# Block solve in four strips of 32 partitions, its scratch in longer runs, and two transfers per pair of head groups, under a new order

## The chip, the core and the metric

The kernel runs on one core of a Trainium2 chip. The metric is the device time of one execution in microseconds; lower is better. Five engines work side by side: PE (TensorE matmuls, with its weight loads shown as PEld), DVE (VectorE), ACT (ScalarE), POOL (GpSimd), and SP, which here only issues DMAs. ACT issues some DMAs too. [...]

## What is computed

```python
for t in range(S):                                  # 768 steps, for 4 x 8 heads of width 40
    y[:, :, t] = einsum('bhd,bhde->bhe', rt, state)
    Sa = einsum('bhde,bhe->bhd', state, at)
    state_decay = state * wt[:, :, None, :] - einsum('bhd,bhe->bhde', Sa, bt)
    state = state_decay + einsum('bhd,bhe->bhde', vt, kt)
x = y.transpose(0, 2, 1, 3).reshape(B * S, H * D)   # 3072 x 320
h = maximum(x @ moe_w_in, 0);  x = (h * h) @ moe_w_out          # 320 -> 2048 -> 320
h = x @ moe2_w_in;  out = where(h > 0, h, exp(min(h, 0)) - 1) @ moe2_w_out
```

All of it is float32: a recurrence over time, then two MLPs.

## The kernel before, in words

**Chunks.** Time is cut into 12 chunks of 64 steps. A chunk's recurrence is done with matrices: `scan`, `prep_a`, `prep_r` and `kb_rows` scale the inputs by running products of w; `planes` and `gram` make a 64 x 64 matrix for each of the 32 heads; the **solve** inverts it; `dyn_f`, `dyn_u`, `dyn_bu`, `dyn_s`, `dyn_y` apply it and carry the state on. Heads go in four groups of eight (`u` = 0 to 3) and two pairs of groups (`p`). The 256 rows of a chunk's y then go through the first MLP (`gemm1` writes `h`, `gemm2` writes `accA` and `accB`), and after the last chunk the second MLP runs chunk by chunk. Values for the MLPs are split into a high and a low part, so each product takes several matmuls: 224 for a chunk and an MLP, 5376 in all. The weights of the first MLP come in 24 pieces (`cs<-w`) that DVE, ACT and PE (`wl`) convert.

**The solve.** A 64 x 64 matrix is inverted by blocks of 16. `gram` stores it to DRAM (`b_scr`, one DMA from ACT for each u). `block_load` (line 997) reads the 128 diagonal blocks, one on each partition (tile `tt`). `block_step` (1009) runs 15 times, two DVE instructions each. `block_store` (1016) sends the inverses through DRAM: transposed through `n_scr` into `nt`, plain through `t_scr` into `tb`. `block_join` (1030) makes the off-diagonal blocks of each 32 x 32 with two stages of 64 small matmuls: stage one `join<-nt,pb` (16 rows, 32 columns, 16 moving), stage two `join<-tb,pb` (32 rows, 16 columns, 16 moving). Each is a float32 matmul, which the trace shows as two instructions with a weight load each, so a stage shows as x128. Stage one's tiles begin at partitions 0 and 32, stage two's at 0 and 32 for half of the heads and at 64 and 96 for the others. Copies on ACT and DVE take the results out of PSUM.

**The order.** No engine's order stands in the text as such. `at` (755) puts each step on a list with a time from three tables (`OFF` by step, `SHIFT` by stage and chunk, `BIAS` by step and chunk); `play` (759) and the class `Order` then lay all instructions out engine by engine with a cost model, the ready instruction of the lowest time first, and `emit` (523) issues them in that order. So every instruction of the main part has line 528 in the profile, and groups are told apart by tile names. Each engine runs its list strictly in order, and a DMA that waits on SP holds up the DMAs behind it.

Of the kernel before, what the change touches and what calls it, by code (L numbers as in the profile page):

```python
# [1459 lines left out]
```

## Time and profile before

| | us |
|---|---|
| median of 3 runs (lowest to highest) | 1325.73 (1323.58 to 1325.76) |
| the profiled execution, its own time | 1321.71 |
| its span, first to last instruction | 1319.9 |
| PE busy in it | 1207.2 |
| mean granted clock of TensorE | 0.949 |

The profiled execution is one run beside the three; its span is 1.8 us shorter than its time and lies inside it. [...]

### The profile page before, as it was taken

How to read it: one execution, taken by the hardware profiler on the slowest of the kernel's cores; microseconds unless marked ns; L12 is line 12 of the kernel's file. 1: busy time of each engine (PE TensorE's matmuls, PEld its weight loads, DVE VectorE, ACT ScalarE, POOL GpSimd, SP SyncE). 2: the span in 40 equal slices, each digit the busy share in tenths (PEclk: the TensorE clock that was granted, in tenths of full speed). 3: DMA queues.
4: the chain of work that ended last, by engine and by line, in shares of the span. 5: the costliest groups of instructions: out<-in, count | busy, mean ns of one | idle time of the engine just before them, and what ended most of it. 6: DMA issues, size and time to landing. Idle time of an engine off the chain costs nothing. (4 is left out here: it accounts for less than half of the span.)

```text
span 1319.9 us, 41548 instructions
## 1 busy us (share of the span) xinstructions
PE 1207.2 (91%) x17409; PEld 1105.7 (84%) x17409; DVE 769.4 (58%) x1434; ACT 792.5 (60%) x1536; POOL 510.3 (39%) x485
## 2 busy tenths in 40 slices
PE   2648779999998999999999999999999999999996
PEld 1536657889897898889888999999999999999995
DVE  6467866756575668665655645578744444444442
ACT  4556576565674657575655546455666666666663
POOL 2341241153363334364334224367633333333332
PEclk9996768897998799999999999999999999999998
DMA  8787786575777475765565434334200010000000
GB/s 268 189 222 207 179 253 153 126 187 150 185 195 164 104 203 130 196 138 160 129 160 136 103 77 135 123 103 124 65 21 20 22 30 21 21 21 22 16 11 18
DMA packets 239570, 157.99 MB, mean 120 GB/s; under 512 B 164112, under 2 KB 212624, under 8 KB 239376
## 3 DMA queue, kind: packets, MB, share of 16 engines
q1 hardware_dynamic: 213072, 148.18, 42.2%
q10 hardware_dynamic: 26304, 7.08, 2.8%
q8 instruction: 139, 2.28, 0.7%
q14 instruction: 55, 0.45, 0.1%
HBM read 114.52 MB, written 40.69 MB: 118 GB/s over the span
## 5 line engine op out<-in xcount | busy, mean ns | idle before, releaser
L528 PE MATMUL h<-xhi,w 128*128 128x256 f32 x1920 | 512.3, 298 | 2.9 <-DVE r L528 1.6
L528 POOL TENSOR_TENSOR glo<-r,ghi 128x512 fp32r<-128x512 f32 x192 | 254.0, 1324 | 413.9 <-ACT ghi L528 219.6
L528 PEld LDWEIGHTS h<-xhi,w 128*128 128x128 f32 x1920 | 357.8, 191 | 22.8 <-DVE r L528 12.7
L528 PE MATMUL h<-xlo,w 128*128 128x256 f32 x1152 | 324.4, 284 | 1.8 <-POOL xlo L528 1.6
L528 PEld LDWEIGHTS h<-xlo,w 128*128 128x128 f32 x1152 | 220.6, 191 | 2.7 <-POOL xlo L528 2.7
L528 ACT ACTIVATE r<-h 128x512 f32<-128x512 f32 x192 | 114.7, 597 | 139.6 <-PE h L528 117.4
L528 DVE SCALAR_TENSOR_TENSOR r<-e,r 128x512 f32<-128x512 f32 x96 | 81.3, 847 | 182.0 <-ACT r L528 180.9
L528 PE MATMUL accA<-w,ghi 128*128 128x320 f32 x768 | 179.1, 315 | 1.9 <-ACT ghi L528 1.9
L528 PE MATMUL accB<-w,ghi 128*128 128x320 f32 x768 | 178.2, 314 | 0.0
L528 DVE TENSOR_TENSOR r<-h,r 128x512 f32<-128x512 f32 x192 | 132.4, 689 | 74.9 <-ACT ghi L528 53.3
L528 PEld LDWEIGHTS accA<-w,ghi 128*128 128x128 f32 x768 | 124.9, 191 | 3.4 <-ACT ghi L528 2.8
L528 PEld LDWEIGHTS accB<-w,ghi 128*128 128x128 f32 x768 | 125.4, 191 | 0.4
L528 PE MATMUL accA<-w,glo 128*128 128x320 f32 x384 | 124.0, 323 | 1.0 <-POOLq L1392 0.6
L528 PE MATMUL accB<-w,glo 128*128 128x320 f32 x384 | 123.2, 321 | 0.0
L528 ACT CAST ghi<-r 128x512 fp32r<-128x512 f32 x96 | 59.0, 615 | 37.2 <-DVE r L528 20.5
L528 DVE SCALAR_TENSOR_TENSOR tt<-tt 128x1 f32<-128x1 f32 (+4 forms) x165 | 71.4, 433 | 15.9 <-DMA tt<-b_scr 8.5
L528 POOL TENSOR_TENSOR kd<-kbt,ks 128x320 f32<-128x320 f32 x42 | 38.1, 908 | 103.1 <-ACT ks L528 101.7
L528 PEld LDWEIGHTS accA<-w,glo 128*128 128x128 f32 x384 | 73.7, 192 | 2.8 <-POOL glo L528 1.1
L528 ACT ACTIVATE ghi<-r 128x512 fp32r<-128x512 f32 x96 | 60.6, 632 | 24.1 <-PE accB L528 21.0
L528 PEld LDWEIGHTS accB<-w,glo 128*128 128x128 f32 x384 | 73.4, 191 | 1.3
L528 ACT ACTIVATE r<-r 128x512 f32<-128x512 f32 x96 | 60.7, 632 | 2.0
L528 ACT COPY gx<-stk 120x1024 bf16<-120x1024 bf16 x48 | 48.5, 1011 | 22.1 <-PE stk L528 13.0
(157 smaller groups left out, 2159.7 us busy)
## 6 DMA issues: line engine op xcount, KB each, us to landing
gy<-ya_scr SPq DMA_DIRECT2D x144, 120.0 KB
rq<-r_scr SPq DMA_DIRECT2D x72, 240.0 KB
cs<-w SPq DMA_DIRECT2D x32, 512.0 KB
kbt<-kbt SPq DMA_DIRECT2D x12, 640.0 KB
cs<-w SPq DMA_DIRECT2D x16, 384.0 KB
b_scr<-bs ACTq DMA_DIRECT2D x48, 128.0 KB
ya_scr<-pl SPq DMA_DIRECT2D x12, 480.0 KB
r_scr<-pl SPq DMA_DIRECT2D x12, 480.0 KB
```

The source lines that it names most:

```text
L528: i = getattr(getattr(self.nc, name), op)(*a, **k)
```

## The change

**Layout of the solve.** The 16 heads of the even groups now lie on partitions 0 to 63 and the 16 of the odd groups on 64 to 127 (`spot`, `side`), so each stage of `block_join` is one group of 64 matmuls that goes round four tiles, at partitions 0, 32, 64 and 96 of both operands and the result. Stage one's result is taken out by one copy on ACT (four copies before), stage two's by four copies on ACT and DVE (eight before). **Scratch.** The work tiles lie in one tile `room` that is cleared once (chunk 1 has its own copy); the inverse is held in rows of 32, so `t_scr` is written in runs of 2 KB (64 bytes before). `n_scr` is now written by two DMAs of ACT in runs of 64 bytes (one DMA in runs of 1 KB before) and read in runs of 1 KB (64 bytes before). The diagonal blocks are read by two DMAs, one for each half of the partitions. **Pairs.** The scale tile `w0` is read, and `x_scr` written, once for two groups of heads; there is now one tile of the double size, where there were two. **Order.** All tables and constants of the planner are new, and its cost model has one more term for DMAs on SP. All instructions move.

```diff
-RP, TB, KB, KS = 1, 3, 3, 1
+RP, TB, KB, KS = 1, 2, 3, 1
...
-T_W2, T_CL = 176.1, 213.4
+T_W2, T_CL = 183.4, 240.8
 OFF = {
-    "scan": -27.03, "pa": -24.12, "pr": -14.35, "kb": -26.05, "pl0": -21.09, "gr0": -19, "pl1": -19.93, "gr1": -18.75, "pl2": -16.7, "gr2": -16.04, "pl3": -16.37, "gr3": -12.38,
+    "scan": -29.65, "pa": -29.52, "pr": -13.98, "kb": -28.54, "pl0": -21.29, "gr0": -19.78, "pl1": -20.36, "gr1": -18.84, "pl2": -16.15, "gr2": -14.86, "bl2": -8.494, "pl3": -16.08,
...
-SWITCH, THIN, CHILL, BUSY = 0.09435, 7.919, 28.43, 0.6976
+SWITCH, THIN, CHILL, BUSY = 0.0005857, 2.68, 1649, 0.6422
...
-CLOSE = 110.0
+CLOSE, HEAVY = 150.0, 0.35
...
-                d += CLOSE
+                d += CLOSE + HEAVY * self.load
+            if o.eng == "SP":
+                self.load = o.runs
...
-    n_scr = [dram.tile([NH, 2, 16, 16], F32, name=f"n_scr{c}") for c in range(NC)]
+    n_scr = [dram.tile([2, 32, NH, 16], F32, name=f"n_scr{c}") for c in range(2)]
...
+        def spot(u):
+            return u % 2 * 2 + u // 2
+
+        def side(g):
+            return slice(g * 2 * HU, (g + 1) * 2 * HU)
...
-            nc.scalar.dma_start(out=ap(b_scr[c][:], u * HU * HB, [[C, C], [HB, HU], [1, C]]), in_=bs[b])
+            nc.scalar.dma_start(out=ap(b_scr[c][:], spot(u) * HU * HB, [[C, C], [HB, HU], [1, C]]), in_=bs[b])
+
+        room = p0.tile([128, 512 + 256 + 1040], F32, name="room")
+
+        def solve_tiles(t):
+            w = t[:, 768:1808]
+            return {
+                "lz": t[:, :512].rearrange("p (n r) -> p n r", r=32), "n1": t[:, 512:768].rearrange("p (n r) -> p n r", r=16),
+                "w0": w[:, :256].rearrange("p (r t) -> p r t", t=16), "w1": w[:, 256:784],
+                "w2": w[:, 784:1040].rearrange("p (r t) -> p r t", t=16)}
+
+        def solve_clear(c):
+            t = ex[c, "s"]
+            nc.gpsimd.memset(flat(t["lz"]), 0.0)
+            nc.gpsimd.memset(t["w1"], 0.0)
+            nc.gpsimd.memset(ap(t["w1"], 16, [t["w1"].ap[0], [33, 16]]), -1.0)
...
+        def block_load(c, g):
+            nc.sync.dma_start(
+                out=ex[c, "s"]["w0"][64 * g:64 * g + 64], in_=ap(b_scr[c][:], g * 2 * HU * HB, [[HB // 4, 64], [C, 16], [1, 16]]))
 
         def block_rest(c):
+            ex[c, "tb"] = p1.tile([128, 2, 2 * HU, 32], F32, tag="tb", bufs=TB, name="tb")
+            for g in range(2):
+                k = g * 2 * HU * HB
+                for o in (0, 32):
+                    nc.sync.dma_start(
+                        out=ex[c, "s"]["lz"][64 * g + o:64 * g + o + 16, :, 16:],
+                        in_=ap(b_scr[c][:], k + o * C + o + 16, [[C, 16], [HB, 2 * HU], [1, 16]]))
+                nc.sync.dma_start(
+                    out=ex[c, "tb"][64 - 64 * g:96 - 64 * g, g], in_=ap(b_scr[c][:], k + 32, [[C, 32], [HB, 2 * HU], [1, 32]]))
+
+        def inverse(c):
+            return ex[c, "s"]["w1"][:, 16:].rearrange("p (r t) -> p r t", t=32)[:, :, :16]
...
         def block_store(c):
-            w = ex[c, "w"]
-            nc.scalar.copy(out=w[:, 0], in_=w[:, 1].rearrange("p r t -> p t r"))
-            nc.scalar.dma_start(out=n_scr[c].rearrange("n h t r -> (n h) t r"), in_=w[::2, 0])
-            for q in range(2):
-                nc.sync.dma_start(out=ap(t_scr[c % 2][:], q * 528, [[1024, 64], [32, 16], [1, 16]]), in_=w[q::2, 1])
+            w, t, n = ex[c, "s"], t_scr[c % 2], n_scr[c % 2]
+            nc.scalar.copy(out=w["w0"], in_=inverse(c).rearrange("p r t -> p t r"))
             for h in range(2):
-                nc.sync.dma_start(out=ex[c, "n1"][32 * h:32 * h + 16], in_=n_scr[c][:, h].rearrange("n t r -> t n r"))
-            for u in range(U):
-                g = u % 2
+                nc.scalar.dma_start(
+                    out=ap(n[:], h * 512 * NH, [[16, NH], [16 * NH, 16], [1, 16]]), in_=w["w0"][2 * h::4])
+            for q in range(2):
+                o = 16 - 16 * q
+                nc.sync.dma_start(out=ap(t[:], 512 * q, [[1024, 64], [1, 512]]), in_=w["w1"][q::2, o:o + 512])
+            for g in range(2):
                 nc.sync.dma_start(
-                    out=ex[c, u // 2, "tb"][64 * g:64 * g + 64, HU * g:HU * g + HU],
-                    in_=t_scr[c % 2][hs(u)].rearrange("n q r t -> (q r) n t"))
+                    out=ex[c, "s"]["n1"][64 * g:64 * g + 64], in_=n[:, :, side(g)].rearrange("h t n x -> (h t) n x"))
+            for g in range(2):
+                nc.sync.dma_start(out=ex[c, "tb"][64 * g:64 * g + 64, g], in_=t[side(g)].rearrange("n q r t -> (q r) n t"))
 
         def block_join(c):
+            s, tb = ex[c, "s"], ex[c, "tb"]
+            lz, x, n1 = s["lz"], s["w2"], s["n1"]
...
+                with nc.group():
+                    for n in range(2 * HU):
+                        for o in range(0, 128, 32):
+                            p = slice(o, o + k)
+                            nc.tensor.matmul(out=ps[o:o + rows, n], lhsT=l(p, n), rhs=r(p, n), start=True, stop=True)
+                return ps
+
+            ps = run(32, 16, lambda p, n: lz[p, n], lambda p, n: n1[p, n])
+            nc.scalar.copy(out=flat(x), in_=flat(ps))
+            ps = run(16, 32, lambda p, n: x[p, n], lambda p, n: tb[p, p.start // 64, n, 16:])
+            for g in range(2):
+                for o in (0, 32):
+                    k = slice(64 * g + o, 64 * g + o + 16)
+                    (nc.vector.tensor_copy if o else nc.scalar.copy)(out=tb[k, g, :, 16:], in_=ps[k])
...
-            w0 = p1.tile([D, HU, C + 1], F32, tag="w0", bufs=W0, name="w0")
-            ex[c, u, "w0"] = w0
-            nc.sync.dma_start(out=w0, in_=p_scr[c][:, hs(u)])
+            if u % 2 == 0:
+                ex[c, u // 2, "w0s"] = p1.tile([D, 2 * HU, C + 1], F32, tag="w0", bufs=W0 // 2, name="w0")
+                nc.sync.dma_start(out=ex[c, u // 2, "w0s"], in_=p_scr[c][:, pair(u)])
+            ex[c, u, "w0"] = ex[c, u // 2, "w0s"][:, hs(u % 2)]
...
-            nc.sync.dma_start(
-                out=x_scr[c][:, 2 * u:2 * u + 2].rearrange("e h (b t) -> e (h b) t", b=B),
-                in_=w0[:, :, :C])
+            if u % 2:
+                nc.sync.dma_start(
+                    out=x_scr[c][:, 2 * u - 2:2 * u + 2].rearrange("e h (b t) -> e (h b) t", b=B),
+                    in_=ex[c, u // 2, "w0s"][:, :, :C])
...
-            for t in t_scr:
-                nc.sync.dma_start(out=t.rearrange("n q r t -> (n q) (r t)"), in_=flat(zero)[:, :512])
+            ex[0, "s"] = solve_tiles(room)
+            solve_clear(0)
+            for t in n_scr:
+                nc.scalar.dma_start(out=ap(t[:], 0, [[256, 128], [1, 256]]), in_=ex[0, "s"]["lz"].rearrange("p n r -> p (n r)")[:, :256])
```

The counts of matmuls don't change. The order of SP falls from 1027 DMAs to 965 (the fallback's included, which isn't run here). Three places show what the new order does.

PE, the joins of chunk 5; first before (`pb`, `nt`, `tb` as above; `y` and `h` belong to earlier chunks):

```order
L528 MATMUL h<-xhi,w_617 128x256
L528 MATMUL h<-xlo,w_617 128x256
L528 MATMUL y<-gh,kbt 40x64 x8
L528 MATMUL join<-nt,pb 32x16 x64
L528 MATMUL join<-tb,pb 16x16 x64
L528 MATMUL h<-xhi,w_446 128x256
L528 MATMUL h<-xlo,w_446 128x256
```

The same place now, the beginning and the end of it (`room` is the new work tile):

```order
L531 MATMUL accB<-w_170,ghi 128x320 x2
L531 MATMUL join<-room 32x16 x64
L531 MATMUL h<-xhi,w_172 128x256
L531 MATMUL h<-xlo,w_172 128x256
...
L531 MATMUL h<-xhi,w_456 128x256
L531 MATMUL h<-xlo,w_456 128x256
L531 MATMUL join<-tb,room 16x16 x64
```

The two stages stood next to each other; now 31 MLP matmuls and six transposes stand between them.

DVE, the end of the block solve of chunk 0, before (`cs` and `ct` are a weight piece in conversion):

```order
L528 TENSOR_REDUCE tt<-tt 128x12
L528 SCALAR_TENSOR_TENSOR cs<-cs 128x512
L528 SCALAR_TENSOR_TENSOR tt<-tt 128x13x13
L528 SCALAR_TENSOR_TENSOR cs<-cs 128x384
L528 TENSOR_REDUCE tt<-tt 128x13
L528 SCALAR_TENSOR_TENSOR tt<-tt 128x14x14
L528 TENSOR_SCALAR ct<-cs 128x512
L528 TENSOR_REDUCE tt<-tt 128x14
L528 SCALAR_TENSOR_TENSOR cs<-cs,ct 128x512
L528 SCALAR_TENSOR_TENSOR tt<-tt 128x15x15
L528 SCALAR_TENSOR_TENSOR cs<-cs 128x512
L528 TENSOR_REDUCE tt<-tt 128x15
```

And now:

```order
L531 TENSOR_REDUCE room<-room 128x12
L531 SCALAR_TENSOR_TENSOR room<-room 128x13x13
L531 TENSOR_REDUCE room<-room 128x13
L531 SCALAR_TENSOR_TENSOR room<-room 128x14x14
L531 TENSOR_REDUCE room<-room 128x14
L531 SCALAR_TENSOR_TENSOR room<-room 128x15x15
L531 TENSOR_SCALAR ct<-cs 128x512
L531 TENSOR_REDUCE room<-room 128x15
```

Between the first step and the last, 16 instructions of other work stood; now 8 do. Ahead of the first step there now stands an instruction `ag<-gram,mask` of chunk 1, which stood among the steps before.

SP, the way back of chunk 0's inverses, before:

```order
L528 DMA t_scr_123<-tt 64x16x16 x2
L528 DMA gy<-ya_scr_89 40x1536 x3
L528 DMA cs<-w 128x1024
L528 DMA p_scr_102<-wx 128x5x130
L528 DMA tb<-t_scr_123 64x8x32
L528 DMA nt<-n_scr_125 16x32x16 x2
```

And now:

```order
L531 DMA t_scr_123<-room 64x512 x2
L531 DMA room<-n_scr_125 64x256 x2
L531 DMA cs<-w 128x1024
L531 DMA tb<-t_scr_123 64x16x32 x2
```

Six DMAs stood between the store of `t_scr` and the read of `n_scr`; now none does.

## Rows read from the trace of the kernel before

**Rows 1.** The page: busy time of each engine, share of the span, instructions.

```profile
PE 1207.2 (91%) x17409; PEld 1105.7 (84%) x17409; DVE 769.4 (58%) x1434; ACT 792.5 (60%) x1536; POOL 510.3 (39%) x485
```

**Rows 2.** Stages: length; busy PE, PEld, DVE, ACT, POOL; PEclk, DMA share, GB/s.

```profile
0.00:100.80 100.80, 44.70 (x383) 34.61 (x383) 57.58 (x105) 52.42 (x103) 36.53 (x44) 1.00 0.80 226
100.80:183.00 82.20, 67.45 (x1400) 51.60 (x1401) 62.39 (x146) 53.03 (x109) 19.07 (x15) 0.67 0.79 210
183.00:300.00 117.00, 106.92 (x2103) 92.80 (x2098) 74.54 (x152) 74.29 (x150) 42.60 (x44) 0.88 0.65 162
300.00:450.00 150.00, 141.09 (x2546) 128.63 (x2543) 98.82 (x208) 86.87 (x173) 66.02 (x62) 0.87 0.64 164
450.00:871.00 421.00, 413.11 (x7793) 378.50 (x7792) 253.95 (x520) 248.22 (x499) 163.44 (x161) 1.00 0.54 138
```

**Rows 3.** Chunk 0, PE in order of time: start, length, shape, count, idle before.

```profile
100.82 3.81 PE L528 MATMUL join<-nt,pb 16*32 16x16 f32 x128 [3.07 <-DMA nt<-n_scr]
```

**Rows 4.** First matmuls of an MLP (h), PE in order of time.

```profile
184.21 0.34 PE L528 MATMUL h<-xhi,w 128*128 128x256 f32 x1
```

**Rows 5.** DVE in order of time, 44 to 92 us: the block solve of chunk 0.

```profile
62.39 0.14 DVE L528 SCALAR_TENSOR_TENSOR tt<-tt 128x1 f32<-128x1 f32 x1
...
85.14 0.43 DVE L528 TENSOR_SCALAR ct<-cs 128x512 uint32<-128x512 uint32 x1 [5.20 <-ACT cs L528]
...
87.40 0.38 DVE L528 TENSOR_REDUCE tt<-tt 128x15 f32<-128x225 f32 x1
```

**Rows 6.** SP queue in order of time, 87 to 101 us.

```profile
87.81 1.41 SPq L528 DMA_DIRECT2D t_scr<-tt  x2
...
93.06 3.03 SPq L528 DMA_DIRECT2D nt<-n_scr  x2
```

**Rows 7.** PE in order of time: second stage of chunk 4, joins of chunk 5.

```profile
293.51 0.26 PE L528 MATMUL join<-tb,pb 32*16 32x16 f32 x7 [1.30 <-issue]
...
418.50 2.25 PE L528 MATMUL join<-nt,pb 16*32 16x16 f32 x128
421.12 1.36 PE L528 MATMUL join<-tb,pb 32*16 32x16 f32 x104 [0.38 <-DVE pb L528]
428.15 0.51 PE L528 MATMUL join<-tb,pb 32*16 32x16 f32 x24 [5.67 <-issue]
```

**Rows 8.** Stretches at and between two drops of PEclk (columns as in rows 2).

```profile
295.10:315.60 20.50, 20.50 (x272) 18.69 (x271) 7.54 (x26) 8.31 (x18) 6.15 (x6) 0.50 0.70 183
315.60:421.40 105.80, 103.57 (x2044) 94.12 (x2045) 76.66 (x149) 67.86 (x131) 51.63 (x50) 1.00 0.68 172
...
435.00:448.70 13.70, 13.70 (x139) 12.52 (x138) 8.36 (x18) 7.04 (x15) 6.70 (x8) 0.50 0.30 74
```

**Rows 9.** PE waits: who waited for what, us, times, longest.

```profile
PE join L528 <- issue: 9.7, 6, 5.7
```

**Rows 10.** PE in order of time, 770 to 795 us: joins between MLP matmuls.

```profile
777.69 0.31 PE L528 MATMUL accB<-w,glo 128*128 128x320 f32 x1
777.83 0.31 PE L528 MATMUL accA<-w,glo 128*128 128x320 f32 x1
...
778.57 0.31 PE L528 MATMUL accB<-w,glo 128*128 128x320 f32 x1
778.81 1.19 PE L528 MATMUL join<-nt,pb 16*32 16x16 f32 x64
779.92 0.41 PE L528 MATMUL accA<-w,glo 128*128 128x320 f32 x1
780.17 0.45 PE L528 MATMUL accB<-w,ghi 128*128 128x320 f32 x2
```

**Rows 11.** Groups by line: copies and what is nearest to them.

```profile
L528 ACT COPY tb<-join 16x128 f32<-16x128 f32 x48 | 12.3, 256 | 29.6 <-PE join L528 19.3 <-DVE tb L528 7.9 <-DMA rq<-r_scr 1.2
L528 ACT CAST xhi<-x2t 128x256 fp32r<-128x256 f32 x36 | 13.2, 369 | 4.5 <-PE x2t L528 3.9 <-PE h L528 0.2
```

**Rows 12.** DMA queues: packets, MB, share of 16 engines.

```profile
q1 hardware_dynamic: 213072, 148.18, 42.2%
```

More of the change, by code (lines that the diff above doesn't have):

```diff
@@ L70 @@
 }
 BIAS = {
-    "scan": [13.26, 6.176, -5.325, 0, -2.635, -5.793, 1.988, 28.93, 1.106, -1.397, -12.63, 8.316],
[107 rows of a table removed]
-    "out": [1.344, -2.018, 20.81, -1.778, 3.498, 62.02, 32.87, 20.64, 20.19, -2.632, 7.53, 18.95],
-    "rg": [-22.09, -29.07, -24.26, -86.91, -107.9, -26.03, -44.44, -5.98, -21.02, -164.5, -37.79, -30.08],
-}
-SWITCH, THIN, CHILL, BUSY = 0.09435, 7.919, 28.43, 0.6976
-YIELD = {"PE": (2.587e+06, 6.959, 80.92), "DVE": (0.1309, 2.937, 5.164e+09), "ACT": (0.2351, 0.03413, 686.2), "POOL": (0.0002282, 4.888, 2.397e+06), "SP": (136.9, 4.725, 220)}
@@ L185 @@
-HOLD = {"PE": (1.841, 924.1), "DVE": (0.7854, 9.898e+05), "ACT": (0.01352, 234.3), "POOL": (1.027e-05, 29.14), "SP": (0, 0.01961)}
-CLOSE = 110.0
+    "scan": [-10.77, 0, 8.671, 22.25, 8.647, 7.543, 7.552, 57.36, -9.983, 1.726, 0.07837, 2.969],
[106 rows of a table added]
+    "out": [-43.42, 10.82, 29.56, 1.722, -17.94, 2.491, 23.86, 32.32, -32.06, -11.42, 32.64, 14.8],
+    "rg": [-69.25, -63.65, -89.85, -123, -54.08, -24.83, -104.6, -87.29, -18.65, -65.62, -35.98, -53.23],
+}
+SWITCH, THIN, CHILL, BUSY = 0.0005857, 2.68, 1649, 0.6422
@@ L187 @@
+YIELD = {"PE": (15.68, 21.3, 50.36), "DVE": (0.08786, 0.1496, 3.675e+09), "ACT": (0.234, 0.007761, 2.477e+09), "POOL": (1.091e-07, 6.404e-08, 1.257e+07), "SP": (1.355e+06, 0.01307, 463.2)}
+HOLD = {"PE": (1.677, 625.8), "DVE": (13.22, 1.071e+09), "ACT": (2599, 0.1083), "POOL": (2.446e-07, 1.967), "SP": (0, 9.838e-07)}
+CLOSE, HEAVY = 150.0, 0.35
 ISSUE, STORE, LOAD, GUARD, COOL, WARM = 350.0, 2100.0, 2100.0, 600.0, 0.40, 0.77
-SLOW = {"b_scr": 300.0, "t_scr": 310.0, "tb": 150.0, "cs": 60.0, "vu": 170.0, "vs": 170.0, "wx": 90.0, "raw": 90.0, "n_scr": 150.0, "out": 160.0, "nt": 100.0, "x": 40.0, "k_scr": 90.0, "a_scr": 80.0, "p_scr": 80.0}
+SLOW = {"b_scr": 240.0, "t_scr": 100.0, "n_scr": 240.0, "room": 50.0, "tb": 150.0, "cs": 60.0, "vu": 170.0, "vs": 170.0, "wx": 90.0, "raw": 90.0, "out": 160.0, "x": 40.0, "k_scr": 90.0, "a_scr": 80.0, "p_scr": 80.0}
@@ L193 @@
 class Op:
-    __slots__ = ("eng", "key", "calls", "dur", "deps", "users", "left", "ready", "end", "start", "tile", "area", "dma", "seq", "kind", "ways", "warm", "cold", "lag", "lock", "label", "event", "late", "wait")
+    __slots__ = ("eng", "key", "calls", "dur", "deps", "users", "left", "ready", "end", "start", "tile", "area", "dma", "seq", "kind", "ways", "warm", "cold", "lag", "lock", "label", "event", "late", "wait", "runs")
 class Order:
@@ L208, in __init__ @@
         self.tail = {"DVE": 0.0, "ACT": 0.0, "SP": 0.0}
+        self.load = 0.0
         self.event, self.label = 0, None
@@ L287, in new @@
         o.tile, o.area, o.dma, o.seq, o.kind = None, 0.0, None, len(self.ops), None
-        o.warm, o.cold, o.lag, o.lock = 0.0, 0.0, 0.0, False
+        o.warm, o.cold, o.lag, o.lock, o.runs = 0.0, 0.0, 0.0, False, 0.0
         self.ops.append(o)
@@ L319, in cost @@
             run = total * size / packets
+            o.runs = packets
             outer = [next((c for _, c in x.ap if c > 1), 1) for x in (out, src)]
@@ L997, in block_load @@
-        def block_load(c):
-            nc.sync.dma_start(out=ex[c, "w"][:, 0], in_=ap(b_scr[c][:], 0, [[HB // 4, 128], [C, 16], [1, 16]]))
-        def block_rest(c):
-            for h in range(2):
-                o = 32 * h
-                nc.sync.dma_start(out=ex[c, "lz"][o:o + 16, :, 16:32], in_=ap(b_scr[c][:], o * C + o + 16, [[C, 16], [HB, NH], [1, 16]]))
-                for g in range(2):
-                    nc.sync.dma_start(
-                        out=ex[c, h, "tb"][64 - 64 * g:96 - 64 * g, HU * g:HU * g + HU],
-                        in_=ap(b_scr[c][:], (2 * h + g) * HU * HB + 32, [[C, 32], [HB, HU], [1, 32]]))
@@ L1009, in block_step @@
-        def block_step(c, t):
-            w = ex[c, "w"]
-            nc.vector.scalar_tensor_tensor(
-                out=w[:, 2, 0:t, 0:t], in0=w[:, 1, 0:t, 0:t], scalar=-1.0,
-                in1=w[:, 0, 0:t, t].unsqueeze(1).to_broadcast([128, t, t]), op0=ALU.mult, op1=ALU.mult)
-            nc.vector.tensor_reduce(out=w[:, 1, 0:t, t], in_=w[:, 2, 0:t, 0:t], axis=AX.X, op=ALU.add)
-        def block_store(c):
-            w = ex[c, "w"]
-            nc.scalar.copy(out=w[:, 0], in_=w[:, 1].rearrange("p r t -> p t r"))
-            nc.scalar.dma_start(out=n_scr[c].rearrange("n h t r -> (n h) t r"), in_=w[::2, 0])
-            for q in range(2):
-                nc.sync.dma_start(out=ap(t_scr[c % 2][:], q * 528, [[1024, 64], [32, 16], [1, 16]]), in_=w[q::2, 1])
-            for h in range(2):
-                nc.sync.dma_start(out=ex[c, "n1"][32 * h:32 * h + 16], in_=n_scr[c][:, h].rearrange("n t r -> t n r"))
-            for u in range(U):
-                g = u % 2
+            nc.scalar.dma_start(out=ap(b_scr[c][:], spot(u) * HU * HB, [[C, C], [HB, HU], [1, C]]), in_=bs[b])
@@ new lines, in inverse, with block_step @@
+        def inverse(c):
+            return ex[c, "s"]["w1"][:, 16:].rearrange("p (r t) -> p r t", t=32)[:, :, :16]
+        def block_step(c, t):
+            w, n = ex[c, "s"], inverse(c)
+            nc.vector.scalar_tensor_tensor(
+                out=w["w2"][:, 0:t, 0:t], in0=n[:, 0:t, 0:t], scalar=-1.0,
+                in1=w["w0"][:, 0:t, t].unsqueeze(1).to_broadcast([128, t, t]), op0=ALU.mult, op1=ALU.mult)
+            nc.vector.tensor_reduce(out=n[:, 0:t, t], in_=w["w2"][:, 0:t, 0:t], axis=AX.X, op=ALU.add)
@@ L1032, in block_join, with run @@
-            x = flat(lz)[:, :NH * 16].rearrange("p (n r) -> p n r", n=NH)
-            def run(rows, put, l, r, evict):
+            s, tb = ex[c, "s"], ex[c, "tb"]
+            lz, x, n1 = s["lz"], s["w2"], s["n1"]
+            def run(rows, k, l, r):
                 if c < 2:
-                    ps = ps_acc.tile([128, NH, 16], F32, tag="accA", name="join")
+                    ps = ps_acc.tile([128, 2 * HU, 16], F32, tag="accA", name="join")
                 else:
-                    ps = ps_at.tile([128, NH, 16], F32, tag="at", name="join")
-                for k in range(2):
-                    with nc.group():
-                        for n in range(16 * k, 16 * k + 16):
-                            for o in (0, 32):
-                                nc.tensor.matmul(out=ps[put(o, n):put(o, n) + rows, n], lhsT=l(o, n), rhs=r(o, n), start=True, stop=True)
-                    evict(ps, k, slice(16 * k, 16 * k + 16))
@@ L1046, in first @@
-            def first(ps, k, n):
-                for g in range(2):
-                    o, m = 64 * g, slice(16 * k + HU * g, 16 * k + HU * g + HU)
-                    (nc.scalar.copy if k else nc.vector.tensor_copy)(out=x[o:o + 64, m], in_=ps[0:64, m])
-            def second(ps, k, n):
-                for g in range(2):
-                    o, m, h = 64 * g, slice(16 * k + HU * g, 16 * k + HU * g + HU), slice(HU * g, HU * g + HU)
-                    nc.scalar.copy(out=ex[c, k, "tb"][o:o + 16, h, 16:32], in_=ps[o:o + 16, m])
-                    nc.vector.tensor_copy(out=ex[c, k, "tb"][o + 32:o + 48, h, 16:32], in_=ps[o + 32:o + 48, m])
@@ L1057, in base @@
-            def base(o, n):
-                return o + 64 * (n // HU % 2)
-            def at_half(o, n):
-                return slice(base(o, n), base(o, n) + 32)
-            run(32, lambda o, n: o, lambda o, n: lz[o:o + 16, n], lambda o, n: n1[o:o + 16, n], first)
-            run(16, base, lambda o, n: x[at_half(o, n), n], lambda o, n: ex[c, n // 16, "tb"][at_half(o, n), n % 16, 16:32], second)
+                    ps = ps_at.tile([128, 2 * HU, 16], F32, tag="at", name="join")
+                with nc.group():
[3 more added lines that the diff above has]
+                            nc.tensor.matmul(out=ps[o:o + rows, n], lhsT=l(p, n), rhs=r(p, n), start=True, stop=True)
@@ L1110, in dyn_u @@
                     for g, r in enumerate(rows):
-                        nc.tensor.matmul(out=ps[r, n], lhsT=tb[r, HU * g + n], rhs=f[r, n], start=True, stop=True)
+                        nc.tensor.matmul(out=ps[r, n], lhsT=tb[r, g, HU * p + n], rhs=f[r, n], start=True, stop=True)
             for g, r in enumerate(rows):
@@ L1116, in dyn_bu @@
         def dyn_bu(c, p):
-            f, tb, ps = ex[c, p, "f"], ex[c, p, "tb"], ex[c, p, "fa"]
+            f, tb, ps = ex[c, p, "f"], ex[c, "tb"], ex[c, p, "fa"]
             with nc.group():
@@ L1122, in dyn_bu @@
                         nc.tensor.matmul(
-                            out=ps[64 * g + 32:64 * g + 64, n], lhsT=tb[k, HU * g + n], rhs=ex[c, 2 * p + g, "vu"][k, n], start=False, stop=(n == HU - 1),
+                            out=ps[64 * g + 32:64 * g + 64, n], lhsT=tb[k, g, HU * p + n], rhs=ex[c, 2 * p + g, "vu"][k, n], start=False, stop=(n == HU - 1),
                             skip_group_check=True)
@@ L1204, in grams @@
                 at("gram", f"gr{u}", c, lambda u=u: gram(c, u))
-            at("gram", "bl3", c, lambda: block_load(c))
+                if u > 1:
+                    at("solve", f"bl{u}", c, lambda u=u: block_load(c, u - 2))
         def solve(c):
```

40 lines of the change are left out of this document (15 added, 25 removed), and 229 rows, old and new, of tables (BIAS, OFF).

## The prediction

> **What bounds the kernel now.** I began with the page's busy times: PE is busy for 1207.2 us, the next engine for 792.5 [rows 1]. So PE is the engine to watch, and 112.7 us of the span of 1319.9 are idle on it. Next I cut the span into stages, to see where. The idle time is not even: 56.1 us of it lie in the first 100.8 us (100.80 less 44.70), 14.8 in the next 82.2, 10.1 and 8.9 in the two stages after, and only 7.9 in the 421 us up to 871 [rows 2]. Up to 183 us the DMA share is 0.79 to 0.80, and PE waits for what the chunks' long chains deliver; the first MLP matmul runs at 184.21 us [rows 4]. From there PE has work at nearly every moment, because MLP matmuls of earlier chunks fill the gaps of the recurrence. There the time is made of three things: how much PE time the matmuls need, the short waits, and the clock, which is 0.88 and 0.87 of full speed on the mean in the stages from 183 to 450 us and 1.00 after that.
>
> So a change of the solve can act in three ways: on PE time in the joins, on waits and clock from 183 to 450 us, and on the chain that starts everything. What DVE, ACT and POOL save after 184 us is hidden by PE.
>
> **The joins' PE time (a).** In chunk 5 stage one takes 2.25 us for 128 matmuls, 17.6 ns each, and stage two 1.36 us for 104, 13.1 ns each [rows 7]. In chunk 0, just as the clock drops, stage one takes 3.81 us, 29.8 ns each [rows 3]. Stage one alternates between two tiles; with four in turn, the same tile comes again after four matmuls. I take stage two's spacing as what it falls to, for it is the nearest row with small tiles in turn: (17.6 - 13.1) x 128 = 0.58 us for a chunk, 7 us for twelve. The bounds: 0 if it stays at 17.6; and if both stages ran at half their spacing (twice as many tiles at work), (8.8 + 6.5) x 128 x 12 = 23.5 us.
>
> [...]
>
> **Going in and out of the small tiles (b).** Between MLP matmuls, `accB` to `accA` takes 0.14 us from start to start (777.69 to 777.83), `accB` to a join 0.24 (778.57 to 778.81), and the first MLP matmul after a join is followed after 0.25 (779.92 to 780.17) [rows 10]. So a stretch of joins costs some 0.2 us beside its matmuls. The order of before has 39 such stretches (most stages are split in two), the new one 23: 16 x 0.2 = 3 us. Below, 0, where a stretch borders on other small tiles anyway.
>
> **Waits and clock (c).** Joins wait on "issue", that is for nothing that the profile shows, six times, 9.7 us in all [rows 9]. The worst is in chunk 5: stage one and two run back to back, then PE stands still for 5.67 us in the middle of stage two [rows 7]. In the order of now 31 MLP matmuls stand between these stages, and only in chunk 0 do two stages still touch. A smaller wait, 1.30 us, stands in chunk 4's second stage, up to 293.51 us [rows 7]. After both the clock drops: to 0.50 for 20.5 us from 295.1 us on, and for 13.7 us from 435.0 us on [rows 8]. At full clock a matmul takes 103.57/2044 = 50.7 ns on the mean of 315 to 421 us, so the 272 matmuls of the first slow stretch would take 13.8 us and the 139 of the second 7.0: 6.7 us lost in each. With the 5.67 us, 19 us hang on these two places. The new order removes what stood around them, but it makes new neighbours elsewhere, so I count a third: 7 us. The bounds: 19, and a loss (the second rival).
>
> **The start (d).** The chain of chunk 0 through the solve: the steps on DVE run from 62.39 to 87.78 us, with 5.20 us of waiting for a weight piece among them [rows 5]; `t_scr` is stored from 87.81, the reads of `n_scr` are issued from 93.06 and take SP 3.03 us [rows 6]; the first join waits for them until 100.82 [rows 3]. Of 16 other instructions among the steps 8 go, at some 0.5 us each (one `ct` takes 0.43): 4 us. The DMAs between store and read go too: the read is issued as soon as `n_scr` has landed. From 87.81 + 1.41 to 93.06 are 3.8 us, of which I count 3, for ACT's copy and store run in that time as well. `t_scr`'s longer runs help the same chain: 64 packets instead of 1024 in each store; at the mean of 0.422 x 16 x 1319.9 us / 213072 = 42 ns a packet on one of 16 DMA engines [rows 12], 960/16 x 42 = 2.5 us, a price that `n_scr`'s store in short runs now pays instead (960 packets more over its two DMAs); these two cancel. Against the sum of 7 stands that the first step is now behind `ag` of chunk 1, which may come a few us later. I take 6 us for the start. Bounds: 0 if `ag` takes it all back; above, the share of DMAs ahead of the first read of `x_scr`: by the orders 33.5 MB where 36.3 stood (five weight pieces fewer), so if the DMAs alone set the start, 7.7% of 184 us, 14 us.
>
> **What I cost at nothing.** One copy of 128 x 256 on ACT in place of four of 64 x 128, and four in place of eight: the nearest rows are 369 ns for 128x256 and 256 ns for 16x128 [rows 11], so ACT gains under 0.5 us for a chunk, beside PE's MLP work; the same copy bare on the chain of chunk 0 costs 0.4 us. The new clearing, once, lies before any data. The pair of groups: `w0` of the next pair now waits for the `x_scr` store of the whole pair, and SP holds what is behind it. After 184 us SP has time and PE has work; without that cover, one such wait is like the 3.03 us of [rows 6], and the start has four of them, 12 us.
>
> **Sum.** 7 + 3 + 7 + 6 = 23 us. The profiled execution's 1321.7 us (span 1319.9 and 1.8 around it) becomes 1298.7; the median of the runs lies 4.0 us above it, so I predict 1325.7 - 23 = **1302.7**, as a median. The likeliest case's own range, with (a) to (d) each some way to its bounds, is 1291 to 1314. No measurement of this kernel tells less than 0.2% (2.7 us) from no change.
>
> **Rivals.**
> - *The four tiles take turns* at PSUM, so that stage one stays at 17.6 ns: (a) is 0, the rest holds, 1310. Against it stands stage two's 13.1 ns; for it, that no row shows four tiles in turn. [...]
> - *Slower: the clock.* After the first MLP matmul, the new order has 13 stretches of 72 or more small matmuls with no MLP matmul or weight conversion among them; that of before has 6. In chunk 5 such a stretch, the two join stages, and the wait in it ran ahead of the slow clock [rows 7, 8]. If (c) gains nothing and four new stretches lose 6.7 us each: 1325.7 - 16 + 27 = 1337. It decides from the third further drop on, which eats the 16 us of (a), (b) and (d). For it, the count; against it, that between 450 and 871 us small matmuls ran among the MLP's too [rows 10] and the mean clock there is 1.00 [rows 2].
> - *No change: the weights.* The last of the 24 weight pieces now stands behind 48.7 MB of DMA, before 45.2. At 162 GB/s [rows 2] that is 21 us later, and chunk 0's MLP can't end without it. If PE waits for 20 us, 23 is eaten: about 1323 to 1326.
> - *More.* (c) gives 19 and (d) 14: 7 + 3 + 19 + 14 = 43, 1283.
>
> **How the numbers follow.** The forecast has 0.50, the turns 0.12, the clock 0.20, the weights 0.10, more 0.08. The range from 1284 to 1336 leaves out about half of the two outer cases, 0.14, and some of their neighbours. Faster: 0.50 + 0.12 + 0.08 = 0.70; a part of the weights' case is within 0.2%, with a little from either side 0.08; slower 0.22.
>
> **What would show it.** (a): stage one's matmuls at 13 ns or so. (b): 23 stretches. (c): no 5.67 us wait near a join, PEclk 1.0 through the joins of chunks 4 and 5. (d): the first join at 94 us or so instead of 100.82, and the first `h` by some 6 us earlier. Wrong would be: a mean clock from 183 to 450 us under the 0.87 of before, or a first `h` that comes later.

## The result: slower by 0.8%, and the profile after

The change takes 1329.8 us in the median of 20 runs (1321.25 to 1346.99), the kernel before 1320.01 in 20 runs beside it (1306.93 to 1327.87): a ratio of **1.0078, with an interval of 1.0054 to 1.0101**, some 10 us slower. I had forecast 1302.7, faster with a chance of 0.70. The time lies in the range of 1284 to 1336, the sign is wrong: from 23 us faster to 10 slower is 33 us.

The profiled execution of after took 1325.97 us with a span of 1323.6, under the median of the 20 runs: its mean granted clock is 0.942, their mean is 0.929. Of the 10 us the profile shows 3.7. The page's busy times (engine, us, share, instructions):

```profile
PE 1188.5 (90%) x17409; PEld 1092.5 (83%) x17409; DVE 751.7 (57%) x1386; ACT 789.8 (60%) x1500; POOL 498.8 (38%) x454
```

Against [rows 1] PE is busy for 18.7 us less: the joins did get cheaper. But the span grew by 3.7, so PE's idle time grew by 22.4 us, from 112.7 to 135.1. The stages, with the columns of [rows 2] (PEclk is the granted clock of TensorE as a share of full speed), show where:

```profile
0.00:100.80 100.80, 47.56 (x592) 36.02 (x593) 64.99 (x114) 53.96 (x107) 34.98 (x41) 0.89 0.81 232
100.80:183.00 82.20, 52.96 (x1067) 43.98 (x1067) 52.52 (x122) 46.16 (x93) 22.07 (x21) 0.69 0.75 194
183.00:300.00 117.00, 109.30 (x1991) 92.74 (x1987) 72.76 (x143) 76.42 (x146) 34.39 (x31) 0.87 0.62 163
300.00:450.00 150.00, 137.99 (x2716) 125.40 (x2716) 88.50 (x176) 86.30 (x170) 58.14 (x52) 0.90 0.63 167
450.00:871.00 421.00, 404.61 (x7818) 370.18 (x7817) 250.08 (x517) 243.20 (x473) 158.52 (x143) 0.99 0.53 139
```

Up to 183 us PE is idle for 53.24 + 29.24 = 82.5 us, before for 70.9. From 183 to 450 it is 19.7 against 19.0. From 450 to 871, where I had left nothing to lose, it is 16.4 against 7.9. The start, on PE in order of time (columns as in [rows 3]):

```profile
94.44 1.44 PE L531 MATMUL join<-room 16*32 16x16 f32 x128
97.72 0.26 PE L531 MATMUL join<-tb,room 32*16 32x16 f32 x10 [1.85 <-ACT room L531]
99.06 1.18 PE L531 MATMUL join<-tb,room 32*16 32x16 f32 x118 [1.08 <-issue]
...
106.19 0.59 PE L531 MATMUL wl<-cs,ident 128*128 128x256 f32 x1 [4.38 <-issue]
...
167.21 2.23 PE L531 MATMUL join<-free 16*32 16x16 f32 x128 [4.72 <-DMA free<-n_scr]
...
207.54 0.58 PE L531 MATMUL h<-xhi,w 128*128 128x256 f32 x1
```

The first join stands at 94.44 us, as forecast (100.82 before, [rows 3]), and takes 1.44 us instead of 3.81. Then the lead is lost: PE stands still for 4.38 us on "issue", chunk 1's joins begin at 167.21, and the first `h` runs at 207.54, where it ran at 184.21 [rows 4]. Chunk 1's late solve goes with the late joins. Its first step on DVE before:

```profile
113.15 0.16 DVE L528 SCALAR_TENSOR_TENSOR free<-free 128x1 f32<-128x1 f32 x1
```

and after:

```profile
130.16 0.16 DVE L531 SCALAR_TENSOR_TENSOR free<-free 128x1 f32<-128x1 f32 x1
```

In the new order the steps stand behind chunk 0's `st` and `vs` on DVE, 17 us later. What PE waited for without a releaser, with the columns of [rows 9]:

```profile
PE y L531 <- issue: 8.0, 4, 3.1
PE join L531 <- issue: 5.2, 5, 2.1
PE wl L531 <- issue: 4.4, 1, 4.4
PE h L531 <- issue: 1.8, 1, 1.8
```

With two smaller groups that is 20.0 us; before it was 9.9, nearly all in joins [rows 9]. The waits have moved out of the joins into what stands behind them, as here in the middle of the run:

```profile
687.10 1.26 PE L531 MATMUL join<-room 16*32 16x16 f32 x128
688.28 0.42 PE L531 MATMUL y<-rf,ss 40*40 40x64 f32 x8
691.82 0.42 PE L531 MATMUL y<-rf,ss 40*40 40x64 f32 x8 [3.11 <-issue]
```

and after chunk 3's second stage, where a slow clock follows as it did in [rows 8]:

```profile
301.78 1.04 PE L531 MATMUL join<-tb,room 32*16 32x16 f32 x101
304.53 0.36 PE L531 MATMUL join<-tb,room 32*16 32x16 f32 x27 [1.71 <-issue]
```

The stretches beside these waits and, in the second line, beside a third (2.08 us, in chunk 4's joins); columns as in [rows 2]:

```profile
306.50:327.00 20.50, 20.50 (x272) 18.75 (x272) 10.73 (x30) 7.74 (x16) 5.33 (x4) 0.50 0.57 157
354.30:364.50 10.20, 9.22 (x84) 8.27 (x84) 3.07 (x5) 3.99 (x8) 1.81 (x4) 0.50 0.45 129
...
692.30:695.70 3.40, 3.40 (x51) 3.13 (x50) 1.26 (x3) 0.42 (x1) 0.00 (x0) 0.50 0.32 68
```

My theory after this: **supply**. Small matmuls at 10 ns use up TensorE's instructions faster than they come, so time saved in a join returns as a wait behind it. The rivals: the new **order** of the start; the **pairs** of `w0` and `x_scr`; the **clock**.

### The profile page after: what moved, and what is told of

The parts are those of the page before. It is cut to its first block, busy times and chain, and to the rows that moved or that the text cites. A ratio compares the mean times of both kernels' runs of the same rounds, so it can differ in the third digit from the quotient of the medians.

```text
span 1323.6 us, 41302 instructions
## 1 busy us (share of the span) xinstructions
PE 1188.5 (90%) x17409; PEld 1092.5 (83%) x17409; DVE 751.7 (57%) x1386; ACT 789.8 (60%) x1500; POOL 498.8 (38%) x454
## 5 line engine op out<-in xcount | busy, mean ns | idle before, releaser
L531 POOL TENSOR_TENSOR glo<-r,ghi 128x512 fp32r<-128x512 f32 x192 | 257.7, 1344 | 469.4 <-ACT ghi L531 214.7
L531 DVE SCALAR_TENSOR_TENSOR r<-e,r 128x512 f32<-128x512 f32 x96 | 77.1, 804 | 179.2 <-ACT r L531 169.9
L531 DVE SCALAR_TENSOR_TENSOR room<-room 128x1 f32<-128x1 f32 (+4 forms) x165 | 70.6, 428 | 17.7 <-DMA room<-b_scr 9.8
L531 PE MATMUL gram<-gy,gx 120*128 120x64 bf16 x1152 | 50.8, 208 | 13.5 <-DMA gy<-ya_scr 7.5
## 6 DMA issues: line engine op xcount, KB each, us to landing
b_scr<-bs ACTq DMA_DIRECT2D x48, 128.0 KB
```

The costliest lines, as they stand in the source:

```text
L531: i = getattr(getattr(self.nc, name), op)(*a, **k)
```

## The experiments

Each was timed against before. Busy, idle (span less busy), issue (all waits on issue) and joins (busy time of their groups) are PE's in the profiled execution, in us. A point is one hundredth of the time of before, some 13 us.

| run | ratio | interval | busy | idle | issue | joins |
|---|---|---|---|---|---|---|
| before | 1 | | 1207.2 | 112.7 | 9.9 | 53.5 |
| after | 1.0078 | 1.0054 to 1.0101 | 1188.5 | 135.1 | 20.0 | 32.4 |
| e1 | 1.0581 | 1.0527 to 1.0635 | 1221.3 | 185.1 | 16.2 | 34.9 |
| e2 | 1.0260 | 1.0204 to 1.0316 | 1215.6 | 128.0 | 9.6 | 55.4 |
| e3 | 1.0121 | 1.0081 to 1.0161 | 1200.6 | 133.3 | 13.3 | 32.9 |
| e4 | 1.0164 | 1.0105 to 1.0222 | 1197.7 | 135.4 | 16.5 | 34.3 |
| e5 | 1.0088 | 1.0050 to 1.0125 | 1206.2 | 118.3 | 11.2 | 48.4 |
| e6 | 1.0221 | 1.0167 to 1.0274 | 1216.8 | 130.5 | 8.8 | 39.5 |
| e7 | 1.0822 | 1.0767 to 1.0877 | 1246.4 | 174.1 | 75.6 | 66.6 |
| e8 | 0.9866 | 0.9814 to 0.9917 | 1166.3 | 128.3 | 1.7 | 16.1 |
| e9 | 0.9881 | 0.9821 to 0.9941 | 1178.4 | 129.3 | 1.3 | 24.5 |
| e10 | 1.0445 | 1.0391 to 1.0499 | 1265.3 | 112.2 | 0.0 | 93.0 |
| e11 | 1.0221 | 1.0163 to 1.0279 | 1195.0 | 132.8 | 28.7 | 39.8 |
| e12 | 1.0039 | 0.9999 to 1.0080 | 1189.5 | 130.6 | 15.8 | 29.0 |
| e13 | 1.0106 | 1.0050 to 1.0163 | 1204.5 | 123.1 | 14.7 | 62.2 |
| e14 | 0.9845 | 0.9792 to 0.9897 | 1161.9 | 125.4 | 5.5 | 19.3 |

**Code and order crossed.** e1 is the new code under the old tables:

```diff
-T_W2, T_CL = 183.4, 240.8
+T_W2, T_CL = 176.1, 213.4
...
+    "bl2": -11.71, "bl3": -11.71, "bn": -58.02, "br": -6.023, "bs": -7.405,
...
-                    at("solve", f"bl{u}", c, lambda u=u: block_load(c, u - 2))
+                    at("gram", f"bl{u}", c, lambda u=u: block_load(c, u - 2))
```

> All of the changed code, but the planner's tables and constants of before (the second half of the block load gets the time of the single load). Theory 'order': the loss lies in the new order of the start, where chunk 1's solve comes 15 us later and the first MLP matmul 23 us later; with the old order the first h is back at 180 to 188 us, the joins keep their 10 ns, and the time is 10 to 20 us under before: ratio 0.985 to 0.993. Theory 'pairs': w0 and x_scr in pairs hold up SP in the start, whatever the order: first h at 200 or later, ratio 1.003 or more. Theory 'clock': the faster joins leave PE with less work and cost clock: half clock for over 150 us in all, ratio about 1.00.

e2 is the old code under the new tables and planner:

```diff
-CLOSE = 110.0
+CLOSE, HEAVY = 150.0, 0.35
...
-            at("gram", "bl3", c, lambda: block_load(c))
+            at("solve", "bl3", c, lambda: block_load(c))
```

> All of the code of before, under the tables, constants and cost model of the change. Theory 'order': first h at 200 us or later, the joins at 13 and 18 ns again, so slower than after: ratio to before 1.012 to 1.025. Theories 'pairs' and 'clock' (the code is at fault): ratio 0.995 to 1.004, first h near 185 us.

e3 undoes the pairs alone:

```diff
-            if u % 2 == 0:
-                ex[c, u // 2, "w0s"] = p1.tile([D, 2 * HU, C + 1], F32, tag="w0", bufs=W0 // 2, name="w0")
...
+            w0 = p1.tile([D, HU, C + 1], F32, tag="w0", bufs=W0, name="w0")
```

> The changed kernel, with w0 read and x_scr written once for each group again (two tiles of single size), under the same tables. Theory 'pairs': first h 10 us or more earlier than 207.5 and ratio to before under 1.000. Theory 'order': first h within 5 us of 207.5, ratio 1.004 to 1.012.

e4 takes the start's times from the old tables:

```diff
+        old = c < 3 and stage not in ("mlp2", "w")
+        off, shift, bias = (OFF_B, SHIFT_B, BIAS_B) if old else (OFF, SHIFT, BIAS)
```

> The changed code; the times of the steps of chunks 0, 1 and 2 come from the old tables, those of the weights and of chunks 3 to 11 from the new ones. Theory 'order', in its narrow form that the start alone costs the loss: first h at 180 to 192 us and ratio to before 0.985 to 0.996. If the order's loss lies after the start: first h early, but the ratio stays at 1.004 or more. Theory 'pairs': first h at 200 us or later all the same.

All four are slower than before, e1 by 5.8%; e1, e2 and e4 are slower than after too, and e3's interval overlaps after's. A table of times fits the code it goes with, and a change of one makes a new order with losses of its own. So crossing can't part code from order here, and "the order is bad, the code is good" is not shown. e3 speaks against the pairs, since undoing them made nothing faster; but its order isn't after's either, for the planner laid it out anew (821 of the 1386 places on DVE hold another instruction). e4 had chunk 1's joins at 156.2 us instead of 167.2, and its first `h` still at 211.6: the narrow form of the theory of the order falls.

What does tell is the column issue: with fast joins (32 to 35 us) it is 13 to 20 us in after, e1, e3 and e4, with joins of 48 to 55 us 10 or 11 in before, e2 and, below, e5, whatever the order. From here on all kernels but e9, e10 and e13 keep after's order, instruction for instruction on all engines (e6 on all but PE); e9 and e13 keep before's. e10 was meant to keep after's and doesn't: the planner prices a small matmul lower behind one of another tile, so it laid e10 out anew. On DVE the order differs from the 116th of 1386 instructions on.

**The joins' pace.** e5 lets two tiles take turns:

```diff
-                    for n in range(2 * HU):
-                        for o in range(0, 128, 32):
+                    for g in range(2):
+                        for n in range(2 * HU):
+                            for o in (64 * g, 64 * g + 32):
```

> The changed kernel in the same order, instruction for instruction; only within a stage of the joins two tiles take turns (first the 32 matmuls of partitions 0 and 32, then the 32 of 64 and 96) where four did. Theory 'supply': TensorE's instructions come in blocks of 16 KB, and the trace shows a block every 3.2 us at the fastest; two tiles in turn take 13 to 18 ns a matmul instead of 10, which leaves the blocks time to come, so the joins' PE time rises from 32 us to 45 to 51, PE's waits fall from 110 us to 95 to 102, and the time to 1.010 to 1.016 of before (after has 1.0078). Theory 'PE time': all of the 13 to 19 us is lost, ratio 1.018 to 1.022. Theory 'the joins don't matter' (the order alone made the loss): 1.006 to 1.010.

e10 lets one tile after the other run:

```diff
-                    for n in range(2 * HU):
-                        for o in range(0, 128, 32):
+                    for o in range(0, 128, 32):
+                        for n in range(2 * HU):
```

> The changed kernel in the same order; in each stage of the joins the 16 matmuls of one tile come in a row, then those of the next. I expect some 25 ns a matmul, so 70 to 85 us of PE time in the joins instead of 32. Theory 'supply': up to about 16 ns a matmul the longer joins replace waits, beyond it they cost; waits fall to 85 to 92 us and the time rises by 20 to 30 us over after: ratio 1.022 to 1.030. Theory 'PE time': all 40 to 50 us show, 1.038 or more. Theory 'the joins don't matter at all': 1.005 to 1.012.

e7 runs each stage twice in place:

```diff
-            for name, op, a, k in o.calls:
+            for name, op, a, k in (o.calls * 2 if o.eng == "PE" and "out" in o.calls[0][3] and "join" in o.calls[0][3]["out"].tensor.name else o.calls):
```

> The changed kernel in the same order, with all 24 stages of joins run twice in place (the second pass writes the same numbers). Theory 'PE time': 24 stages at 1.26 us are 30 us more, ratio 1.029 to 1.033. Theory 'supply': 24 more blocks of 256 instructions, each of which takes 3.2 to 5 us to come where small matmuls stand close together, so 60 to 100 us more less what slack there was: ratio 1.04 to 1.08, and PE's waits on issue over 50 us.

The joins' groups by line in after (busy, mean ns of one, idle before them and its releasers):

```profile
L531 PE MATMUL join<-room 16*32 16x16 f32 x1408 | 14.9, 181 | 2.4 <-issue 2.2 <-DMA room<-n_scr 0.2
L531 PE MATMUL join<-tb,room 32*16 32x16 f32 x1408 | 14.1, 177 | 4.8 <-issue 3.0 <-ACT room L531 1.9
```

in e5:

```profile
L531 PE MATMUL join<-room 16*32 16x16 f32 x1408 | 24.7, 181 | 1.5 <-issue 1.5
L531 PE MATMUL join<-tb,room 32*16 32x16 f32 x1408 | 19.1, 174 | 2.1 <-ACT room L531 1.5 <-issue 0.5
```

and in e10:

```profile
L531 PE MATMUL join<-room 16*32 16x16 f32 x1408 | 49.6, 186 | 0.0
L531 PE MATMUL join<-tb,room 32*16 32x16 f32 x1408 | 35.2, 175 | 1.6 <-ACT room L531 1.6
```

In e5 the joins take 16.0 us more and PE's idle time falls by 16.8: the ratio moves by 0.1 points, less than the interval. So what four tiles save over two is worth nothing that can be told from 0 in this order. In e10 the waits on issue are gone (0.0). Its joins take 44.6 us more than e5's, and it costs 3.6 points, 47 us, more; but with an order of its own and a mean clock of 0.912 in its profile, against 0.932 in e5's, it doesn't show that each microsecond of slower joins counts. In e7 the joins take 34.2 us more than in after and waits on issue 55.6 more, 89.8 together; the time rose by 7.4 points, 98 us.

The ratios alone didn't decide for supply. e5's, 1.0088, is under what I had written for it and inside the range of "the joins don't matter"; e10's, 1.0445, is in the range of "PE time"; e7's is just over the range of supply. The waits decide. e7 shows them, on PE in order of time:

```profile
93.38 1.34 PE L531 MATMUL join<-room 16*32 16x16 f32 x138
97.35 1.79 PE L531 MATMUL join<-room 16*32 16x16 f32 x118 [2.62 <-issue]
99.61 0.28 PE L531 MATMUL join<-tb,room 32*16 32x16 f32 x10 [0.47 <-ACT room L531]
103.15 1.25 PE L531 MATMUL join<-tb,room 32*16 32x16 f32 x128 [3.26 <-issue]
107.15 1.18 PE L531 MATMUL join<-tb,room 32*16 32x16 f32 x118 [2.75 <-issue]
```

From wait to wait there are 118 + 10 = 128 matmuls, then 128 again, each with a weight load: 256 instructions. The page's row of the instruction queue (packets, MB, share) is in after

```profile
q8 instruction: 139, 2.28, 0.7%
```

in e7

```profile
q8 instruction: 163, 2.67, 0.8%
```

and in e8, below,

```profile
q8 instruction: 127, 2.08, 0.7%
```

e7 has 3072 matmuls and 3072 weight loads more, which is 24 times 256, and 24 packets more; e8 has half of these fewer, and 12 packets fewer. So a packet of 16 KB carries 256 of TensorE's instructions, and where small matmuls stand close PE waits for the next packet at the end of one. The trace also has the time of each packet, which settles it. In e7 packets of this queue landed at 95.65, 101.77 and 105.76 us, and PE went on at 97.35, 103.15 and 107.15 in the rows above, 1.4 to 1.7 us behind each. The same holds for all 48 waits on issue of 0.4 us or more in before, after and e7: PE goes on 1.2 to 1.7 us after a packet has landed, behind the 5.67 us of [rows 7] too (landed at 426.89, on at 428.15). And packets come slowly: in these three profiles no two start less than 3.16 us apart. By the means of the rows above 128 matmuls with their loads, one packet, take 1.3 us in after's joins, 1.7 to 2.2 in e5's and 3.2 to 4.5 in e10's, which has no such wait; at the 50.7 ns of the prediction it is 6.5.

Ahead of after's 5376 MLP matmuls the waits on issue come to 2.0 us in all; ahead of its 3072 matmuls of the joins they come to 5.2, and one of those in the rows of e7 takes 3.26 us.

**Fewer instructions.** e8 reads the joins' numbers as bfloat16, which is less precise, in one matmul and one load for two of each:

```diff
+                if op == "matmul" and "join" in k["out"].tensor.name:
+                    k = dict(k, lhsT=k["lhsT"].bitcast(BF16)[:, 1::2], rhs=k["rhs"].bitcast(BF16)[:, 1::2])
```

> The changed kernel in the same order; the joins' matmuls read the upper halves of their float32 numbers as bfloat16, which is less precise, and takes one matmul and one weight load where two of each stood. So 64 matmuls a stage instead of 128, 3072 PE instructions of each kind fewer in all halves of the joins. Theory 'PE time': the joins take 16 us instead of 32, ratio 0.995 to 0.998. Theory 'supply': besides these 16 us, 8 us or more of waits on issue go, ratio 0.986 to 0.992.

e9 has the same lines in the kernel before, under its own order.

> The kernel before, in its order, with the joins' numbers read as bfloat16 in one pass as in the run e8_one_pass. Theory 'supply': the joins' 51 us of PE time fall to 25 and their 10 us of waits on issue to under 3, so the old code and order gain as much as the new ones did from it or more: ratio 0.974 to 0.984, under e8's 0.987. Theory 'the new layout is better and was only held back by the supply': ratio 0.988 to 0.995, over e8's.

e8 lies at 0.9866, in the range of the theory of supply: joins 16.3 us less, waits on issue 18.3 less. e9, at 0.9881, is outside what I had written for supply and at the edge of the range for "the new layout is better", with an interval that reaches into both: with waits on issue nearly gone (1.3), old and new are the same within their intervals, so it decides for neither. In e9 the joins take 29.0 us less, yet PE's idle time rises by 16.6, by waits on other engines' results and DMAs. So supply isn't all that can eat PE time saved.

**Spreading.** e6 cuts the joins into pieces and pulls MLP matmuls that could run already between them:

```diff
+        self.spread(made)
         for o in sorted(made, key=lambda o: (o.start, o.seq)):
```

> The changed kernel in its order, but on PE the joins are cut into up to six pieces, and three MLP matmul groups that could run already and stood behind the join are put between each two pieces; all other engines keep their order. Some 40 more stretches of joins. Theory 'supply': the instruction waits behind the joins from 280 us on go, PE's waits on issue fall from 20 us to 12 or less, ratio 1.000 to 1.005. My step (b) (0.2 us for each stretch of small tiles): 40 more stretches cost 8 us, ratio 1.012 to 1.015. If both hold, they cancel near 1.007.

Waits on issue fell to 8.8 as expected, but the time rose by 1.4 points over after, over twice the 8 us that my 0.2 us for a stretch makes and outside both ranges. PE is busy for 28.3 us more, of which only 7.1 in joins. The mean clock of its runs is 0.925. I take it that the MLP matmuls pulled ahead are missing later, where small matmuls then stand alone; that is argued, not shown.

**The start.** e11 runs the joins of chunks 0 and 1 alone twice, as in e7 but with `o.label[2] < 2`, and e13 does the same in before. e12 gives these two chunks the one pass of e8, and e14 gives it to the other ten.

> The changed kernel in the same order, with the joins of chunks 0 and 1 alone run twice in place, which puts off the first h by some 8 us. It asks what a late start costs, step (d) of my prediction. If the start sets the time: ratio 1.013 to 1.017. If PE makes up for a late start before 450 us, as the traces of before and after look: ratio 1.006 to 1.010.

> The changed kernel in the same order; the joins of chunks 0 and 1 alone read bfloat16 halves in one pass (4 of 24 stages). The run e8 with all 24 gained 2.1 points over the change. If the start weighs no more than its share, 4/24 of that: ratio 1.003 to 1.006. If the start sets the time, because every us there comes before all else: first h at 200 to 204 us, ratio 0.996 to 1.002.

> The kernel before in its order, with the joins of chunks 0 and 1 run twice in place, some 8 to 10 us of PE time and waits more ahead of the first h. If a late start costs what it is late, or more: first h at 190 us or later, ratio 1.006 to 1.015. If PE makes up for it by 450 us: 0.998 to 1.004.

> The changed kernel in the same order; the joins of chunks 2 to 11 in one pass, those of chunks 0 and 1 as in the change. If the start weighs no more than its share: 20/24 of the 2.1 points are gained here, ratio 0.988 to 0.993. If the start sets the time: 0.993 to 0.999.

In the start PE time and waits do show. e13: joins 8.7 us more and issue 4.8 more make 13.5; 1.06% of before is 14. e11: 7.4 and 8.7 make 16.1, measured 1.43 points over after, 19 us. The sizes are rough: e13's interval goes from 0.50 to 1.63%, e11's runs from 1330 to 1360 us, and the spans of their profiles grew by 7.7 and 4.2 us only. e12's gain of 0.4 points over after is its share of e8 but within the intervals; e14 gains 2.3 points, as much as all 24 stages did, within the intervals. So the start isn't where one pass gains most; the joins of chunks 2 to 11 are. The first `h` is at 201.4 us in e12, 201.6 in e14, whose joins of chunks 0 and 1 are after's own, and 202.9 in e5. So some of after's 207.54 is chance of one execution; the other 17 us or more over 184.21 stay whatever the pace of the joins, so they belong to the order.

## Why the prediction was wrong

**(a) failed in its kind, not in its size; (c) and (d) failed in their signs, and they are the larger part of the miss.** e5 tells them apart. It is the change without what four tiles save, and it is as slow as the change (0.1 points between them, uncertain by some 0.4). So (a) was worth about 0 where I forecast 7 us, and all the rest, (b), (c) and (d) with what I costed at nothing, came out 0.5 to 1.25% slower, some 12 us, where I forecast 16 faster.

**(a)** I priced 7 us of PE time, with a bound of 23.5; the profile gives 21.1 (53.5 to 32.4). Stage one's spacing in chunk 0 is 1.44 us over 128, 11 ns. The rival of turns is out: four tiles take 10 to 11 ns a matmul where two took 14 to 18 in e5. What failed is the sentence that PE's own time is what the stages after 183 us are made of, so that time saved there is time saved. I put the instructions' own arrival at nothing. In e5 16.0 us of joins come back, 16.8 us of PE's idle time go, and the time stays.

**(b)** can't be told by itself: the 23 stretches are there, but no run changes their number without changing waits or clock.

**(c)** has the wrong sign. The 5.67 us wait of [rows 7] is gone, but waits on issue doubled from 9.9 to 20.0, and the clock drops of 20.5 and 10.2 us come again in other places. I had taken such waits for accidents of two stages that touch. They are waits for the next packet of instructions, and they grew with the joins' pace: 0.0 us with one tile after the other (e10, in its own order), 11.2 with two in turn (e5), 20.0 with four (after), and 75.6 where each stage with four ran twice (e7).

**(d)** has the wrong sign in its milestone. The first join came 6.4 us earlier, as worked out, but I costed only chunk 0's chain. The first `h` waits on PE behind chunk 1's dynamic steps (from the end of chunk 1's joins to it are 33.5 us, before 20.6), and chunk 1's solve began 17 us later; I had seen that `ag` of chunk 1 moved and gave it "a few us". PE's idle time up to 183 us grew by 11.6 us in after and by 5.4 in e5. The milestone was poor too: by 450 us after has run 6366 matmuls where before had run 6432 [rows 2], 66 fewer, or 3.3 us at 50.7 ns (an estimate). Of my two signs of being wrong the later `h` came; the other did not, for the clock from 183 to 450 us is 0.87 and 0.90 where it was 0.88 and 0.87.

**What I costed at nothing** held as far as tried: the pairs (e3, in an order of its own) and the weights (after 210 us no wait of PE is on a weight piece). Of the rivals the clock came nearest, with 1337; 1.0078 times the 1325.7 of before is 1336. That is in part luck. The mean clock is lower, 0.929 over after's runs, where before's runs beside the experiments have 0.943 to 0.949. But the four further slow stretches after the first `h` that made the 1337 are not in the profile: between 183 and 871 us PE ran at 0.5 for 72 us in both kernels.

**What stays open.** e5's joins are nearly as slow as before's (48.4 us and 53.5), and it is still 0.9% slower. In its profile that is 4.6 us of span; it has 5.6 us more idle time than before, 5.4 of them up to 183 us. With that goes a lower clock (0.925 over its runs). Its stages, with the columns of [rows 2], have it in the start and behind 450 us, where before had 1.00:

```profile
0.00:100.80 100.80, 48.49 (x595) 36.75 (x596) 66.18 (x117) 55.38 (x109) 35.03 (x41) 0.80 0.81 235
100.80:183.00 82.20, 58.20 (x1111) 47.09 (x1110) 57.98 (x127) 48.44 (x98) 22.13 (x22) 0.68 0.78 198
...
450.00:871.00 421.00, 411.42 (x7529) 377.36 (x7526) 236.37 (x485) 231.62 (x448) 149.70 (x133) 0.94 0.51 134
```

I have not shown what lowers it, nor which part of the new order makes these 0.9%.

## What to carry to other kernels

Before pricing a gain in small matmuls by their PE time, count the instructions: where bursts of 256 in 1.3 us stood close, as in e7, waits of 2.62 to 3.26 us came behind them, and fewer instructions helped (e8, 0.9866) where faster ones didn't (after, 1.0078, against e5, 1.0088). Slow the piece down in the same order and see whether the time moves; it costs one run and says what a gain there is worth. Where a table of times sets the order, a change crossed with the old table tells nothing of its parts, so freeze the order, change one thing inside it, and compare the two orders, for a planner can take the change as a reason for a new one, as it did in e10.
